# First batch's loads issued up front, transposes in three PSUM banks, a new split of the attention sums, and one held gate tile in an attention + gated-FFN kernel

## The chip, the cores and the metric

The kernel runs on one core of one Trainium2 chip. The metric is device time in microseconds (us), the median of several executions. Where a time within the kernel is given (such as "at 60.86 us"), it is read from one profiled execution and counts from the start of its span. The profiled span is about 1.7 us shorter than the device time.

## The reference, cut to what matters

```python
B, H, S, Nb, D = 8, 8, 576, 16, 64            # inputs float32
k_all = concatenate([beacon_k, k]); v_all = concatenate([beacon_v, v])      # 592 keys per head
scores = q @ k_all.T / sqrt(D)                # causal mask on the 576, never on the beacons
attn = softmax(scores) @ v_all                # per batch and head
x = attn.transpose(0, 2, 1, 3).reshape(B * S, H * D)                        # 4608 tokens x 512
out = (gelu(x @ w_gate) * (x @ w_val)) @ w_out                              # d_ff = 1536
```

## The kernel before

It works batch by batch: attention of batch b (four head pairs), then one 512-token chunk of gate and value work (12 tiles of 8 matmuls). The out-projection of the previous chunk (48 matmuls, "units", `o(n)`) is strewn through the attention, as filler while ScalarE computes the exps. Meanwhile GpSimd issues the casting loads of q, k and v for batch b+1, and SyncE issues ten DMA transposes that turn q and k into `qkT`, the operand of the scores.

The kernel's PSUM tiles take eight banks: `s` twice two banks (scores, gate/value tiles), `z` two banks, `x` one, `o` one.

```python
def attend(b, m, acc, c0, sums, q0, q1, start=True):       # columns q0..q1 of a pair's queries
    ...                                                    # per key tile and head one matmul:
    mm(acc[...], ones if sums else v_sb, expT, ...)

def sums(b, m):                                            # softmax sums, and the last 64 queries' values
    z_ps = psum_x.tile([P, 1024], FP32, tag="z")
    attend(b, m, z_ps, Z0 + Z_SPLIT, True, Z_SPLIT, S)     # 10 matmuls
    attend(b, m, z_ps, 0, False, X_SPLIT, S)               # 10 matmuls of 64 columns (X_SPLIT = 512)
    attend(b, m, z_ps, Z0, True, 0, Z_SPLIT, start=False)  # 2
def values(b, m):
    x_ps = psum_x.tile([P, X_SPLIT], FP32, tag="x")
    attend(b, m, x_ps, 0, False, 0, X_SPLIT)               # 10

def gate_val_first(ci, n=0):
    for fi in range(2):                                    # two tiles: both "s" buffers held
        gate_val_mms(ci, fi, range(K_CHUNKS - 1))
    o(n)                                                   # filler until the last pair is scaled
    for fi in range(2):
        gate_val_mms(ci, fi, [K_CHUNKS - 1])
        gate_val_end(ci, fi)                               # gelu on ScalarE, product on VectorE

# ... start: values first, then q/k runs
load_v_fp32(0)                                             # SyncE queue, fp32, cast later
heat(10)
load_runs(0, 2); load_beacon(dma, bk0, beacon_k[0]); ...; load_runs(2, 4)   # GpSimd queue
attention(0, "S0 r2 S1 k1 S2 q1 S3 r3 w0",                 # k, q: TensorE transposes through bank o
    "c024 S0 c13 S1 Z k2 I S2 V q2 w1 M S3", "S0 S1 Z k3 I w2 S2 V q3 M S3 w3",
    "S01 Z S2 V S3", "Z V", ...)                           # S scores, Z sums, I invert, V values, M scale
load_qk(1); load_v(1)                                      # r load q/k runs, w weights, c cast values
gate_val_first(0); xbar_transpose(1); gate_val(0, 2, F_TILES)
for b in range(1, B):
    if b == 1:   attention(b, "S0 L S1 S23", ..., "S0 S1 Z S2 V S3 O12", "Z V")  # L: w_out, O: units
    elif b == 2: attention(b, "S01 O12 S23 O12", "S01 Z V O12 S23 O12", ..., "Z V")   # 84 units
    else:        attention(b, "O4 S01 O8 S23 O2", "S01 Z V S23 O10", "S01 Z V S23 O12", "S01 Z V S23 O8", "Z V")
    load_qk(b + 1); load_v(b + 1)                          # (if b + 1 < B)
    gate_val_first(b, 4 if b > 2 else 0)
    xbar_transpose(b + 1)                                  # ten DMA transposes on SyncE
    gate_val(b, 2, F_TILES)
for fi in range(F_TILES): gate_val(8, fi, fi + 1); o(4)    # last chunk
o(OUT_UNITS)
```

The softmax here doesn't subtract the row's maximum and nothing guards it: scores larger than these inputs give would overflow.

Of the kernel before, what the change touches and what calls it, by code (L numbers as in the profile page):

```python
# [43 lines left out]
X_SPLIT = 512  # L44
Z0, Z_SPLIT = 448, 64
# [12 lines left out]
def kernel(  # L58
# [85 lines left out]
    def load_qk(b):  # L144

        qt, kt = q_ring[b % 2], k_ring[b % 2]
        load_beacon(dma, kt[0:NB, 0, :], beacon_k[b])

        def rows(dst, src):
            dma(dst.rearrange("p (h d) -> p h d", d=D), src.rearrange("h p d -> p h d"))  # L150

        for j in range(5):
            r0, n = (NB, 112) if j == 0 else (0, KROWS[j])
            rows(kt[r0 : r0 + n, j, :], k[b, :, S_LO[j] : S_LO[j] + n, :])
            n = min(P, S - j * P)
            rows(qt[0:n, j, :], q[b, :, j * P : j * P + n, :])
# [18 lines left out]
    def load_v_fp32(b):  # L175
        def start(o, i):
            keep(nc.sync.dma_start(out=o, in_=i))

        load_beacon(start, flat(v32)[0:NB, 0, :], beacon_v[b])
        for t in AV_ORDER:  # L180
            r0, n = (NB, 112) if t == 0 else (0, KROWS[t])
            start(v32[r0 : r0 + n, t, :, :], v[b, :, S_LO[t] : S_LO[t] + n, :].rearrange("h p d -> p h d"))

# [21 lines left out]
    def heat(n):  # L205
        t = psum_o.tile([P, CH], FP32, name="heat", tag="o")
        for _ in range(n):
            mm(t, warm[:, 0:P], warm, True, True)
# [31 lines left out]
    def trans_o(m, w, copy=None):  # L240
        t_ps = psum_o.tile([P, 1024], BF16, name="t_ps", tag="o")
        trans(m, w, t_ps, [(S, copy or dve_copy)])
# [56 lines left out]
    def sums(b, m):  # L299
        z_ps = z_of[b * NPAIR + m] = psum_x.tile([P, 1024], FP32, name="z_ps", tag="z")  # L300
        attend(b, m, z_ps, Z0 + Z_SPLIT, True, Z_SPLIT, S)
        attend(b, m, z_ps, 0, False, X_SPLIT, S)
        attend(b, m, z_ps, Z0, True, 0, Z_SPLIT, start=False)

    def values(b, m):
        x_ps = x_of[b * NPAIR + m] = psum_x.tile([P, X_SPLIT], FP32, name="x_ps", tag="x")
        attend(b, m, x_ps, 0, False, 0, X_SPLIT)

# [17 lines left out]
    def scale(b, m):  # L326
        i = b * NPAIR + m
        rec = rec_of.pop(i)
        del exp_of[i]
        for acc, q0, q1 in ((z_of.pop(i), X_SPLIT, S), (x_of.pop(i), 0, X_SPLIT)):  # L330
            keep(
                nc.vector.tensor_tensor(  # L332
                    out=xT_sb[:, m, b * S + q0 : b * S + q1],
                    in0=acc[:, 0 : q1 - q0],
                    in1=rec[:, q0:q1],
                    op=ALU.mult,
                )
            )
# [35 lines left out]
    def gate_val_first(ci, n=0):  # L374

        for fi in range(2):
            gate_val_mms(ci, fi, range(K_CHUNKS - 1))
        o(n)
        for fi in range(2):
            gate_val_mms(ci, fi, [K_CHUNKS - 1])  # L380
            gate_val_end(ci, fi)
# [31 lines left out]
    def attention(b, *slots, extra=None):  # L413


        for m, slot in enumerate(slots):
            for step in slot.split():
# [3 lines left out]
                elif kind == "Z":  # L421
                    sums(b, m - 1)
                    if "I" not in slot:
                        invert(b, m - 1)
                elif kind == "I":
                    invert(b, m - 1)
                elif kind == "V":
                    values(b, m - 1)
                    if "M" not in slot:
                        scale(b, m - 1)  # L430
                elif kind == "M":
                    scale(b, m - 1)
                elif kind == "O":
                    o(int(n))
                else:
                    extra[kind](*n)
# [4 lines left out]
    load_v_fp32(0)  # L441
# [15 lines left out]
    for w, copies in ((0, [(S, dve_copy)]), (1, [(114, act_copy), (S, act_copy)])):  # L457
        t0 = psum_s.tile([P, 2048], BF16, name="t0_ps", tag="s")
        trans(0, w, t0, copies)

    W_CUT = ((0, 256), (256, 512), (512, 1024), (1024, 1536))
    extra = {
        "k": lambda m: trans_o(int(m), 1),
        "q": lambda m: trans_o(int(m), 0),
        "c": lambda *tt: cast_v(0, *(int(t) for t in tt)),
        "r": lambda m: load_runs(2 * int(m), 2 * int(m) + 2),
        "w": lambda i: load_gate_val(*W_CUT[int(i)]),
# [3 lines left out]
        "S0 r2 S1 k1 S2 q1 S3 r3 w0", "c024 S0 c13 S1 Z k2 I S2 V q2 w1 M S3", "S0 S1 Z k3 I w2 S2 V q3 M S3 w3", "S01 Z S2 V S3", "Z V",  # L471
        extra=extra,
    )
    load_qk(1)
    load_v(1)
    gelu_table()
    gate_val_first(0)
# [3 lines left out]
    extra["L"] = load_out_w  # L481
    for b in range(1, B):
        exp_table()
        if b == 1:
            attention(b, "S0 L S1 S23", "S0 S1 Z S2 V S3", "S0 S1 Z S2 V S3", "S0 S1 Z S2 V S3 O12", "Z V", extra=extra)
        elif b == 2:
            attention(b, "S01 O12 S23 O12", "S01 Z V O12 S23 O12", "S01 Z V O12 S23 O12", "S01 Z V S23 O12", "Z V")
        else:
            attention(b, "O4 S01 O8 S23 O2", "S01 Z V S23 O10", "S01 Z V S23 O12", "S01 Z V S23 O8", "Z V")
# [4 lines left out]
        gate_val_first(b, 0 if b == 1 else 4 if b>2 else 0)  # L494
        if b + 1 < B:
            xbar_transpose(b + 1)
        gate_val(b, 2, F_TILES)
# [34 lines left out]
```

## Time and profile before

| | before |
|---|---|
| median time (three runs) | 426.18 us (426.07 to 426.87) |
| TensorE busy (profile, part 1) | 387.8 of 425.5 us, 91% |
| first scores / first gate matmul of batch 0 | 10.98 / 34.31 us |
| first scores of batch 1 | 59.36 us |
| first gate matmul of batches 1, 2, 3, 7 | 78.96, 132.56, 176.13, 353.30 us |
| batches 3 to 7, mean period | 44.3 us |

The occupancy rows of the profile (40 slices of 10.6 us, busy tenths; PEclk is the granted TensorE clock in tenths) show where TensorE has room: only at the front.

```profile
PE   5778958898999999999999999999999999999985
PEclk9589988999999999999999999999999999999999
```

The digits 5, 7, 7, 8 stand for batch 0, the 5 in the sixth slice is the wait before batch 1, and the PEclk digits 5 and 8 beside them say that the clock was also lowered there.

The waits view gives, for each pair of waiter and releaser, the total us, the count and the longest.

```profile
PE gv_ps L200 <- DVE hT_sb L364: 7.8, 8, 1.0
PE s_ps L200 <- DMA qkT<-q_sb: 3.5, 2, 3.0
```

The first line is a stall of 0.98 us in each of the eight batches: the third gate tile finds both PSUM buffers held. The second is small: transposed q is awaited for 3.0 us before batch 1 and 0.5 us once more.

The chain of work that ended last (start, us, what) names what set the pace at the front.

```profile
2.77 6.93 DMA bk<-in_beacon_k_dram
...
33.36 6.75 DMA k_sb<-in_k_dram
...
54.55 4.83 DMA qkT<-q_sb
59.38 0.39 PE s_ps L200 x2
```

Batch 1's chain is a load of k issued at 33.36 us (landing behind the weights at 40.1), ten transposes on SyncE, the last of which lands 4.8 us after its issue, and then the scores.

### The profile page before, as it was taken

To read this page: it belongs to the slowest core of one execution; us is meant where nothing else is said; L and a number is where in the kernel's file an instruction comes from. 1 tells how busy PE (TensorE), PEld (TensorE's weight loads), DVE (VectorE), ACT (ScalarE), POOL (GpSimd) and SP (SyncE) were. 2 spreads that over 40 slices of the span, in tenths; PEclk is the share of its full clock that TensorE was granted. 3 is DMA by queue.
4 is the path that set the end of the run, shared out by engine and by line. 5 is a ranking of instruction groups with operands and counts; after the bars stand their busy time and mean duration, and the time that the engine had idled before them with its cause. 6 is when DMAs were issued, how large, how long until landed. Compare 5 with 4: busy or idle time off the path is not lost.

```text
span 425.5 us, 7034 instructions
## 1 busy us (share of the span) xinstructions
PE 387.8 (91%) x2814; PEld 180.0 (42%) x2814; DVE 190.8 (45%) x324; ACT 188.6 (44%) x255; POOL 169.4 (40%) x302
## 2 busy tenths in 40 slices
PE   5778958898999999999999999999999999999985
PEld 2444424443444434444444444444544444444432
DVE  1565316533346335643564436444654365433321
ACT  1653368235343356435743476237723762322200
POOL 3868424930229504760468035813491230000000
PEclk9589988999999999999999999999999999999999
DMA  9599999995219991799149901991199310000111
GB/s 159 80 169 183 138 85 147 113 139 56 75 62 98 145 79 51 71 161 103 50 48 150 138 30 51 143 157 29 51 129 141 65 52 27 0 2 25 49 51 74
DMA packets 153041, 38.02 MB, mean 89 GB/s; under 512 B 141232, under 2 KB 148400, under 8 KB 153008
## 3 DMA queue, kind: packets, MB, share of 16 engines
q0 software_dynamic: 108048, 18.54, 64.7%
q1 hardware_dynamic: 44960, 19.03, 24.1%
q8 instruction: 22, 0.36, 0.4%
q14 instruction: 11, 0.09, 0.1%
HBM read 38.27 MB, written 9.44 MB: 112 GB/s over the span
## 4 chain that ended last, share of the span: by engine, by line
PE 71%; DMA 11%; SPq 7%; DVE 6%; ACT 3%; issue 2%; POOL 1%; DVEq 0%; ACTq 0%; POOLq 0%
PE gv_ps L200 33%; PE o_ps L200 22%; PE z_ps L200 7%; PE s_ps L200 6%; SPq L162 4%; PE x_ps L200 4%; DMA wo_sb<-in_moe_w_out_dram 3%; SPq L165 3%; DMA qkT<-q_sb 3%; DVE o_sb L402 2%; DVE hT_sb L364 2%; ACT ge_sb L203 2%; DMA bk<-in_beacon_k_dram 2%; DMA k_sb<-in_k_dram 2%; DMA qkT<-k_sb 1%
## 5 line engine op out<-in xcount | busy, mean ns | idle before, releaser
L203 ACT ACTIVATE ge_sb<-gv_ps 128x512 bf16<-128x512 f32 x108 | 63.6, 597 | 162.1 <-PE gv_ps L200 162.1
L271 POOL TENSOR_SCALAR_AFFINE_SELECT expT<-expT 128x256 bf16<-128x256 bf16 (+2 forms) x160 | 60.1, 387 | 168.5 <-ACT expT L203 168.2
L364 DVE TENSOR_TENSOR hT_sb<-gv_ps,ge_sb 128x512 bf16<-128x512 f32 x108 | 74.0, 691 | 117.4 <-ACT ge_sb L203 117.4
L203 ACT ACTIVATE expT<-s_ps 128x1024 bf16<-128x1024 f32 (+3 forms) x128 | 103.7, 862 | 46.8 <-PE s_ps L200 45.5
L200 PE MATMUL gv_ps<-xT_sb,wg_sb 128*128 128x512 bf16 x432 | 113.5, 379 | 7.8 <-DVE hT_sb L364 7.8
L200 PE MATMUL gv_ps<-xT_sb,wv_sb 128*128 128x512 bf16 x432 | 113.5, 379 | 0.0
L200 PE MATMUL o_ps<-wo_sb,hT_sb 128*128 128x512 bf16 x432 | 103.1, 379 | 7.0 <-DVE o_sb L402 6.2
L200 PEld LDWEIGHTS <-wg_sb 128*128 128x128 bf16 x432 | 41.6, 98 | 60.0 <-issue 11.8
L200 PEld LDWEIGHTS <-hT_sb 128*128 128x128 bf16 x432 | 40.2, 98 | 55.8 <-issue 11.6
L200 PEld LDWEIGHTS <-wv_sb 128*128 128x128 bf16 x432 | 42.3, 98 | 51.0
L200 PE MATMUL s_ps<-qkT 64*128 64x80 bf16 (+5 forms) x384 | 41.3, 296 | 12.6 <-DMA qkT<-q_sb 3.5
L402 DVE COPY o_sb<-o_ps 128x512 f32<-128x512 f32 x36 | 24.9, 691 | 53.9 <-PE o_ps L200 53.9
L315 DVE STREAM_TRANSPOSE zt<-z_ps 128x576 f32<-128x576 f32 x32 | 25.0, 782 | 40.6 <-PE z_ps L200 40.6
L200 PE MATMUL z_ps<-expT,ones 128*64 128x464 bf16 (+5 forms) x384 | 36.2, 300 | 1.1 <-DVE xT_sb L332 1.1
L112 POOL DMA_DIRECT2D v_sb<-in_v_dram x35 | 29.7, 869 | 10.9 <-DMA k_sb<-in_k_dram 5.7
L200 PEld LDWEIGHTS <-qkT 64*128 64x128 bf16 x384 | 14.7, 95 | 42.9 <-issue 28.9
L112 POOL DMA_DIRECT2D k_sb<-in_k_dram x35 | 30.2, 864 | 1.0 <-DMA wv_sb<-in_moe_w_val_dram 1.0
L112 POOL DMA_DIRECT2D q_sb<-in_q_dram x35 | 30.6, 874 | 0.0
L200 PEld LDWEIGHTS <-v_sb 128*64 128x64 bf16 (+1 forms) x640 | 22.0, 114 | 8.4 <-issue 2.6
L320 DVE STREAM_TRANSPOSE rec<-rz 128x576 f32<-128x576 f32 x32 | 24.9, 778 | 1.1
L200 PE MATMUL x_ps<-expT,v_sb 128*64 128x512 bf16 (+4 forms) x320 | 25.4, 285 | 0.0
L200 PEld LDWEIGHTS <-ones 128*64 128x64 bf16 (+1 forms) x384 | 17.6, 114 | 13.6 <-issue 9.0
(34 smaller groups left out, 115.4 us busy)
## 6 DMA issues: line engine op xcount, KB each, us to landing
out_dram<-o_sb SPq DMA_DIRECT2D x36, 256.0 KB, 2.0
q_sb<-in_q_dram POOLq DMA_DIRECT2D x28, 128.0 KB, 6.0
k_sb<-in_k_dram POOLq DMA_DIRECT2D x21, 128.0 KB, 6.1
v_sb<-in_v_dram POOLq DMA_DIRECT2D x21, 128.0 KB, 10.4
wo_sb<-in_moe_w_out_dram POOLq DMA_DIRECT2D x1, 1536.0 KB, 13.4
wg_sb<-in_moe_w_gate_dram POOLq DMA_DIRECT2D x2, 512.0 KB, 7.0
wv_sb<-in_moe_w_val_dram POOLq DMA_DIRECT2D x2, 512.0 KB, 8.9
k_sb<-in_k_dram POOLq DMA_DIRECT2D x7, 112.0 KB, 3.4
```

The source lines that it names most:

```text
L112: keep(nc.gpsimd.dma_start(out=out_ap, in_=in_ap))
L162: keep(nc.sync.dma_start_transpose(out=qkT[:, 1, :, j * P : j * P + n], in_=kt[0:n, j, :]))
L165: keep(nc.sync.dma_start_transpose(out=qkT[:, 0, :, c : c + n], in_=qt[0:n, j, :]))
L200: keep(nc.tensor.matmul(out_ap, lhsT, rhs, start=start, stop=stop, **kw))
L203: keep(nc.scalar.activation(out_ap, in_ap, func, **kw))
L271: nc.gpsimd.affine_select(out=d, in_=d, pattern=[[0, 2], [1, DIAG[t]]], compare_op=ALU.is_ge, fill=0.0, base=NB if t == 0 else 0, channel_ ...
L315: keep(nc.vector.transpose(zt, z_of[i][:, Z0 : Z0 + S]))
L320: nc.vector.transpose(rec.rearrange("p (n j) -> p n j", j=32), rz.unsqueeze(2).to_broadcast([P, NBLK, 32]))
L364: nc.vector.tensor_tensor(out=h_of[ci][:, fi, :], in0=gv_ps[:, 1, :], in1=ge_sb, op=ALU.mult)
L402: keep(nc.vector.tensor_copy(o_sb, o_ps))
```

## The change: its intent, and the diff

1. **First batch.** All q and k runs are loaded first; the fp32 values follow behind (a one-element GpSimd write to their tile holds SyncE back), and two of the five value tiles come by GpSimd's casting queue. TensorE's transposes rotate through banks o, x and z, one pair ahead. The weights come in three slices instead of four. A few warm-up matmuls keep the clock up.
2. **Output weights** (`L`) are loaded before batch 1's first scores instead of after them.
3. **Out-projections** move: batch 1 takes 24 units instead of 12, batch 2 60 instead of 84, the tail 12 more; batches 3 to 7 keep 48.
4. **One gate tile held** in batches 1 to 7 instead of two, with up to 7 units as filler.
5. **New split.** The first 64 queries, not the last 64, sit beside the sums. Only one key tile reaches them, so ten small matmuls become two.

In the schedule strings of the changed kernel, a digit after Z, I, V or M names the pair, `o` or `x` after k1, q1 and so on the PSUM bank, `y3` loads value tile 3 by GpSimd, and `N1` issues the next waiting load of batch 1.

```diff
-X_SPLIT = 512
-Z0, Z_SPLIT = 448, 64
+SPLIT = 64
+Z0 = 448
 ...
     def sums(b, m):
-        attend(b, m, z_ps, Z0 + Z_SPLIT, True, Z_SPLIT, S)
-        attend(b, m, z_ps, 0, False, X_SPLIT, S)
-        attend(b, m, z_ps, Z0, True, 0, Z_SPLIT, start=False)
+        attend(b, m, z_ps, Z0, True, 0, SPLIT)
+        attend(b, m, z_ps, Z0 + SPLIT, True, SPLIT, S)
+        attend(b, m, z_ps, 0, False, 0, SPLIT, start=False)
     def values(b, m):
-        attend(b, m, x_ps, 0, False, 0, X_SPLIT)
+        attend(b, m, x_ps, 0, False, SPLIT, S)
 ...
-    def gate_val_first(ci, n=0):
-        for fi in range(2):
+    def gate_val_first(ci, fill, n, tiles=1):
+        for fi in range(tiles):
             gate_val_mms(ci, fi, range(K_CHUNKS - 1))
-        o(n)
-        for fi in range(2):
+        fill(n)
+        for fi in range(tiles):
 ...
-    load_v_fp32(0)
     heat(10)
     load_runs(0, 2)
 ...
     load_runs(2, 4)
+    load_runs(4, 6)
+    load_runs(6, 8)
+    keep(nc.gpsimd.memset(v32[0:1, :, 0, 0:1], 0.0))
+    load_v_fp32(0)
 ...
-    W_CUT = ((0, 256), (256, 512), (512, 1024), (1024, 1536))
+    W_CUT = ((0, 512), (512, 1024), (1024, 1536))
     attention(0,
-        "S0 r2 S1 k1 S2 q1 S3 r3 w0", "c024 S0 c13 S1 Z k2 I S2 V q2 w1 M S3", "S0 S1 Z k3 I w2 S2 V q3 M S3 w3", "S01 Z S2 V S3", "Z V",
+        "S0 k1o q1x S1 S2 q2o S3 k2x y3 y4", "w0 N1 S0 c0 Z0 S1 S2 S3", "w1 I0 k3x c2 S0 c1 S1 q3o V0 M0 Z1 S2 V1 S3", "I1 S0 M1 S1 Z2 S2 S3 I2 V2 M2", "Z3 I3 V3 w2 M3",
 ...
-    gate_val_first(0)
+    gate_val_first(0, heat, 2, 2)
 ...
-            attention(b, "S0 L S1 S23", "S0 S1 Z S2 V S3", "S0 S1 Z S2 V S3", "S0 S1 Z S2 V S3 O12", "Z V", extra=extra)
+            attention(b, "L S0 S1 S2 S3", "S0 S1 Z0 S2 I0 S3 V0", "M0 Z1 S0 S1 O7 S2 V1 I1 S3 M1", "S0 Z2 S1 I2 V2 S2 S3 M2 O5", "Z3 I3 V3 M3 O12", extra=extra)
 ...                                    # batch 2 likewise, 84 units -> 60
-            attention(b, "O4 S01 O8 S23 O2", "S01 Z V S23 O10", "S01 Z V S23 O12", "S01 Z V S23 O8", "Z V")
+            attention(b, "O5 S0 S1 O7 S2 S3 O2", "S0 S1 Z0 I0 V0 S2 M0 S3 O10", "S0 S1 Z1 V1 I1 S2 S3 M1 O12", "S0 S1 Z2 V2 I2 M2 S2 S3 O5", "Z3 I3 V3 M3")
 ...
-        gate_val_first(b, 0 if b == 1 else 4 if b>2 else 0)
+        gate_val_first(b, o, 0 if b == 1 else 0 if b == 2 else 7)
 ...
-        gate_val(b, 2, F_TILES)
+        gate_val(b, 1, F_TILES)
+    o((N_CHUNKS - 2) * OUT_UNITS - out_done[0])
```

More of the change, by code (lines that the diff above doesn't have):

```diff
@@ L142, in load_beacon, with qk_loads, load_qk @@
         start(dst.rearrange("p (h d) -> p h d", d=D), src.rearrange("h p d -> p h d"))
-    def load_qk(b):
+    def qk_loads(b):
         qt, kt = q_ring[b % 2], k_ring[b % 2]
-        load_beacon(dma, kt[0:NB, 0, :], beacon_k[b])
         def rows(dst, src):
-            dma(dst.rearrange("p (h d) -> p h d", d=D), src.rearrange("h p d -> p h d"))
+            return dst.rearrange("p (h d) -> p h d", d=D), src.rearrange("h p d -> p h d")
+        loads = [rows(kt[0:NB, 0, :], beacon_k[b])]
         for j in range(5):
             r0, n = (NB, 112) if j == 0 else (0, KROWS[j])
-            rows(kt[r0 : r0 + n, j, :], k[b, :, S_LO[j] : S_LO[j] + n, :])
+            loads.append(rows(kt[r0 : r0 + n, j, :], k[b, :, S_LO[j] : S_LO[j] + n, :]))
             n = min(P, S - j * P)
-            rows(qt[0:n, j, :], q[b, :, j * P : j * P + n, :])
+            loads.append(rows(qt[0:n, j, :], q[b, :, j * P : j * P + n, :]))
+        return loads
+    def load_qk(b):
+        for out_ap, in_ap in qk_loads(b):
+            dma(out_ap, in_ap)
     def xbar_transpose(b):
@@ L179, in load_v_fp32, with load_v_tile @@
         load_beacon(start, flat(v32)[0:NB, 0, :], beacon_v[b])
-        for t in AV_ORDER:
+        for t in (0, 2, 1):
             r0, n = (NB, 112) if t == 0 else (0, KROWS[t])
             start(v32[r0 : r0 + n, t, :, :], v[b, :, S_LO[t] : S_LO[t] + n, :].rearrange("h p d -> p h d"))
+    def load_v_tile(b, t):
+        dma(v_ring[b % 2][0 : KROWS[t], t, :, :], v[b, :, S_LO[t] : S_LO[t] + KROWS[t], :].rearrange("h p d -> p h d"))
     def cast_v(b, *tiles):
@@ L203, in act, with bank, heat @@
         keep(nc.scalar.activation(out_ap, in_ap, func, **kw))
-    def heat(n):
-        t = psum_o.tile([P, CH], FP32, name="heat", tag="o")
+    def bank(tag, dtype, n, name):
+        pool = psum_o if tag == "o" else psum_x
+        if tag == "z":
+            n *= 2
+        return pool.tile([P, n], dtype, name=name, tag=tag)
+    def heat(n, tag="o"):
+        if n == 0:
+            return
+        t = bank(tag, FP32, CH, "heat")
         for _ in range(n):
-            mm(t, warm[:, 0:P], warm, True, True)
+            mm(t[:, 0:CH], warm[:, 0:P], warm, True, True)
     def tr(out_ap, in_ap):
@@ L238, in act_copy, with trans_in @@
         keep(nc.scalar.copy(o, i))
-    def trans_o(m, w, copy=None):
-        t_ps = psum_o.tile([P, 1024], BF16, name="t_ps", tag="o")
+    def trans_in(tag, m, w, copy=None):
+        t_ps = bank(tag, BF16, 1024, "t_ps")
         trans(m, w, t_ps, [(S, copy or dve_copy)])
@@ L300, in sums @@
         z_ps = z_of[b * NPAIR + m] = psum_x.tile([P, 1024], FP32, name="z_ps", tag="z")
-        attend(b, m, z_ps, Z0 + Z_SPLIT, True, Z_SPLIT, S)
-        attend(b, m, z_ps, 0, False, X_SPLIT, S)
-        attend(b, m, z_ps, Z0, True, 0, Z_SPLIT, start=False)
+        attend(b, m, z_ps, Z0, True, 0, SPLIT)
+        attend(b, m, z_ps, Z0 + SPLIT, True, SPLIT, S)
+        attend(b, m, z_ps, 0, False, 0, SPLIT, start=False)
     def values(b, m):
-        x_ps = x_of[b * NPAIR + m] = psum_x.tile([P, X_SPLIT], FP32, name="x_ps", tag="x")
-        attend(b, m, x_ps, 0, False, 0, X_SPLIT)
+        x_ps = x_of[b * NPAIR + m] = psum_x.tile([P, S - SPLIT], FP32, name="x_ps", tag="x")
+        attend(b, m, x_ps, 0, False, SPLIT, S)
     rec_of = {}
@@ L329, in scale @@
         del exp_of[i]
-        for acc, q0, q1 in ((z_of.pop(i), X_SPLIT, S), (x_of.pop(i), 0, X_SPLIT)):
+        for acc, q0, q1 in ((z_of.pop(i), 0, SPLIT), (x_of.pop(i), SPLIT, S)):
             keep(
@@ L421, in attention @@
                 elif kind == "Z":
-                    sums(b, m - 1)
-                    if "I" not in slot:
+                    sums(b, int(n or m - 1))
+                    if not n:
                         invert(b, m - 1)
                 elif kind == "I":
-                    invert(b, m - 1)
+                    invert(b, int(n))
                 elif kind == "V":
-                    values(b, m - 1)
-                    if "M" not in slot:
+                    values(b, int(n or m - 1))
+                    if not n:
                         scale(b, m - 1)
                 elif kind == "M":
-                    scale(b, m - 1)
+                    scale(b, int(n))
                 elif kind == "O":
@@ L435, in attention @@
                 else:
-                    extra[kind](*n)
+                    extra[kind](*n) if kind in "kqcrwLhy" else extra[kind](n)
     exp_table()
-    load_v_fp32(0)
     heat(10)
@@ L456, with load_next @@
     load_runs(2, 4)
-    for w, copies in ((0, [(S, dve_copy)]), (1, [(114, act_copy), (S, act_copy)])):
+    load_runs(4, 6)
+    load_runs(6, 8)
+    keep(nc.gpsimd.memset(v32[0:1, :, 0, 0:1], 0.0))
+    load_v_fp32(0)
+    for w, copies, n in ((0, [(S, dve_copy)], 0), (1, [(114, act_copy), (S, act_copy)], 3)):
         t0 = psum_s.tile([P, 2048], BF16, name="t0_ps", tag="s")
         trans(0, w, t0, copies)
-    W_CUT = ((0, 256), (256, 512), (512, 1024), (1024, 1536))
+        heat(n)
+    queue = qk_loads(1)
+    def load_next(n):
+        for _ in range(min(n, len(queue))):
+            dma(*queue.pop(0))
+    W_CUT = ((0, 512), (512, 1024), (1024, 1536))
     extra = {
-        "k": lambda m: trans_o(int(m), 1),
-        "q": lambda m: trans_o(int(m), 0),
+        "k": lambda m, tag: trans_in(tag, int(m), 1),
+        "q": lambda m, tag: trans_in(tag, int(m), 0),
         "c": lambda *tt: cast_v(0, *(int(t) for t in tt)),
         "r": lambda m: load_runs(2 * int(m), 2 * int(m) + 2),
+        "h": lambda n, tag: heat(int(n), tag),
+        "L": lambda: load_out_w(),
+        "y": lambda t: load_v_tile(0, int(t)),
+        "X": lambda n: load_v(1),
+        "N": lambda n: load_next(int(n)),
         "w": lambda i: load_gate_val(*W_CUT[int(i)]),
@@ L470 @@
         0,
-        "S0 r2 S1 k1 S2 q1 S3 r3 w0", "c024 S0 c13 S1 Z k2 I S2 V q2 w1 M S3", "S0 S1 Z k3 I w2 S2 V q3 M S3 w3", "S01 Z S2 V S3", "Z V",
+        "S0 k1o q1x S1 S2 q2o S3 k2x y3 y4", "w0 N1 S0 c0 Z0 S1 S2 S3", "w1 I0 k3x c2 S0 c1 S1 q3o V0 M0 Z1 S2 V1 S3", "I1 S0 M1 S1 Z2 S2 S3 I2 V2 M2", "Z3 I3 V3 w2 M3",
         extra=extra,
     )
-    load_qk(1)
+    load_next(99)
     load_v(1)
     gelu_table()
-    gate_val_first(0)
+    gate_val_first(0, heat, 2, 2)
     xbar_transpose(1)
     gate_val(0, 2, F_TILES)
-    extra["L"] = load_out_w
     for b in range(1, B):
@@ L484 @@
         if b == 1:
-            attention(b, "S0 L S1 S23", "S0 S1 Z S2 V S3", "S0 S1 Z S2 V S3", "S0 S1 Z S2 V S3 O12", "Z V", extra=extra)
+            attention(b, "L S0 S1 S2 S3", "S0 S1 Z0 S2 I0 S3 V0", "M0 Z1 S0 S1 O7 S2 V1 I1 S3 M1", "S0 Z2 S1 I2 V2 S2 S3 M2 O5", "Z3 I3 V3 M3 O12", extra=extra)
         elif b == 2:
-            attention(b, "S01 O12 S23 O12", "S01 Z V O12 S23 O12", "S01 Z V O12 S23 O12", "S01 Z V S23 O12", "Z V")
+            attention(b, "S0 O12 S1 S2 O12 S3", "S0 Z0 I0 S1 S2 O12 S3 V0 M0", "S0 S1 Z1 I1 V1 S2 S3 O6", "S0 S1 M1 Z2 V2 S2 S3 O4 I2 M2", "O2 Z3 V3 I3 M3 O12", extra=extra)
         else:
-            attention(b, "O4 S01 O8 S23 O2", "S01 Z V S23 O10", "S01 Z V S23 O12", "S01 Z V S23 O8", "Z V")
+            attention(b, "O5 S0 S1 O7 S2 S3 O2", "S0 S1 Z0 I0 V0 S2 M0 S3 O10", "S0 S1 Z1 V1 I1 S2 S3 M1 O12", "S0 S1 Z2 V2 I2 M2 S2 S3 O5", "Z3 I3 V3 M3")
         gelu_table()
```

## The prediction

> **What bounds the kernel now.** TensorE. By the profile's first part it is busy 387.8 of 425.5 us; from batch 3 on, batches repeat every 44.2 us with it nearly full. The losses:
> - Start (timeline): the first scores run at 10.98 us, because the beacon keys issued at 2.77 us land 6.93 us later, among the fp32 value loads. The exps of batch 0 go from 11.63 to 32.40 us, 20.8 us for about 14 us of work (862 ns x 16): they wait for transposes that pass one by one through one PSUM bank. Gate work starts at 34.31.
> - Batch 1 starts at 59.36 us after 3.0 us of waiting for transposed q, whose chain begins with loads landing behind the weights (40.14 us). The clock is at half for 9.0-19.3, 22.7-26.1 and 60.2-67.0 us.
> - Each batch: 0.98 us where the third gate tile waits for a PSUM buffer, since two are held open (waits: 8 times, 7.8 us).
> - Batch 2: 84 out-projection units, with stalls (1.09 + 3 x 0.39 us).
>
> **What the change is worth.**
> 1. q/k runs first, values behind them. A q or k load alone landed in 3.1 us (6-7 under the value loads); my estimate for the first scores is 7.3 us, 3.5 earlier. Transposes in three banks, one pair ahead, let ScalarE run nearly without gaps (perhaps 5 more): last exp near 24, gate work near 25.5. The warm-up matmuls should avoid the half-clock stretch from 9 us. The Trainium skill, "TensorE: Matmul & The Clock Gate", Part 1, says that the clock drops after an idle window of about 3.4 us; the clock records agree (stretches of 3.4, 6.8, 10.2 us).
> 2. But batch 1 is tied to DMA: 3.1 MB of weights at the 205 GB/s seen, 11 loads, ten DMA transposes (19.2 us from first issue to last landing). The weights start some 4 us earlier. The output weights now load beside the transposes; the Trainium skill, "DMA: Bandwidth & Descriptors", "Issuing engines are not separate DMA queues", says that these share the 16 engines, so I charge 1-2 us. Batch 1 starts at about 53.5: **-5.9**. TensorE still waits there some 5 us; the clock still drops.
> 3. Out-projections: batch 1 takes 24 units instead of 12 in the same time (filling waits), batch 2 60 instead of 84 (-5.2, and -1.8 of stalls), the tail 12 more (+2.6).
> 4. One held gate tile in batches 1-7: 7 x 0.98 = **-6.9**.
> 5. The split saves 8 matmuls per pair: ten 64-column ones (0.15 us together, timeline) become two; the large group keeps about 0.7 us. -0.12 x 24 pairs where TensorE is the limit = **-2.9**.
> 6. Score waits at batch starts: -1.0. New waits (scores for exps, transposed keys; slack there is about 1 us): +1.2.
>
> Sum -19.9: 426.2 becomes **407 us**, with 400 to 414 holding it 8 times in 10. Faster by over 2%: 0.95; within 2%: 0.045; slower: 0.005.
>
> **What would show it.** First scores near 7 us; last exp of batch 0 near 24; batch 1's first scores at 52-55 after a DMA wait; period near 42.4 us; the 0.98 us gate stalls gone but for batch 0's; z and x groups 0.12 us shorter per pair.
>
> **What would make it wrong.** Output weights delaying the transposes so that batch 1 starts near 59 as before (+5); later batches limited by the DMA chain, the stalls reappearing as waits for transposed keys.

## The result, and the profile after

The changed kernel takes 419.54 us (median of 4, 419.40 to 420.15) against 426.36 us for the kernel before in the same rounds. The ratio is 0.9842, with a 95% interval of 0.9824 to 0.9859. Ratios here and below are the mean time of one kernel's fast runs over that of the other's of the same rounds, so they are not quite the ratio of the quoted medians. The change is a gain of 1.6%; 407 us, or 4.5%, had been predicted.

Marks read from the timelines (first gate matmul of a batch, and the scores that open batch 1) divide the difference:

| stretch | before | after | difference | predicted |
|---|---|---|---|---|
| start to gate of batch 0 | 34.31 | 28.21 | -6.1 | -8.8 |
| start to the scores of batch 1 with all data | 59.36 | 60.86 | +1.5 | -5.9 |
| from there to gate of batch 1 | 19.6 | 20.1 | +0.5 | 0 |
| gate of batch 1 to gate of batch 2 | 53.6 | 45.4 | -8.2 | about -8.5 |
| gate of batch 2 to gate of batch 7 | 220.7 | 217.0 | -3.8 | about -7 |
| gate of batch 7 to the end | 72.2 | 74.4 | +2.2 | about +1.6 |

The first row is part of the second; rows two to six sum to -7.8 us, against the -19.9 of the prediction. (The last column sorts the terms of its sum by row. The fifth is five stalls, 4.9, and 20 pairs of the split, 2.4, less 0.2 for waits; the period of 42.4 us that the prediction also names would make it -9.) Most of the miss of 12 us is in two rows, 7.4 us before batch 1 and about 3 us in batches 2 to 6; the other three are off by 0.3 to 0.6 us each. Batch 0 did get 6.1 us faster, and all of it is lost again before batch 1.

The occupancy rows of the changed kernel:

```profile
PE   7789819999999989998999999989999999999975
PEclk9899967999999999999999999999999999999999
```

The third and fourth digit rose to 8 and 9, but the sixth, before batch 1, fell from 5 to 1, and PEclk stands at 6 and 7 there.

The waits view:

```profile
PE s_ps L209 <- DMA qkT<-q_sb: 7.4, 5, 3.3
PE s_ps L209 <- issue: 6.2, 1, 6.2
PE gv_ps L209 <- DVE hT_sb L382: 1.0, 1, 1.0
```

The gate stall went from 7.8 us in 8 to 1.0 in 1, just as intended. What grew is the wait for transposed q, from 3.5 us in 2 to 7.4 in 5, and one of 6.2 us which the view cannot attribute ("issue"). The stretch itself shows what that one is (timeline of TensorE and SyncE, 50 to 62 us; lines between left out):

```profile
49.65 1.03 PE L209 MATMUL gv_ps<-xT_sb,wv_sb 128*128 128x512 bf16 x4
...
51.05 1.20 SPq L171 DMA_TRANSPOSE qkT<-q_sb  x1
...
56.91 0.61 PE L209 MATMUL s_ps<-qkT 64*128 64x512 bf16 x2 [6.23 <-issue]
...
60.86 0.97 PE L209 MATMUL s_ps<-qkT 64*128 64x64 bf16 x8 [3.35 <-DMA qkT<-q_sb]
```

Gate work of batch 0 ends at 50.7 us, and TensorE then waits 6.23 and 3.35 us. The chain of the changed kernel for this stretch:

```profile
28.00 8.81 DMA k_sb<-in_k_dram
36.83 1.30 SPq L168
...
51.05 9.77 DMA qkT<-q_sb
```

The load of k was issued 5.4 us earlier than before but landed only 3.3 us earlier, at 36.8. The last transpose took 9.77 us to land where it had taken 4.83. The clock was lowered for longer, too: half speed from 54.5 to 68.1 us, 13.7 us, against 6.8 us before (60.2 to 67.0).

In batches 3 to 7 the removed stalls came back as waits of another name. TensorE's waits at the head of batches 3, 4, 6 and 7 (start of the matmul, us, and in brackets the idle time before it):

```profile
149.58 0.38 PE L209 MATMUL s_ps<-qkT 64*128 64x64 bf16 x6 [0.94 <-DMA qkT<-q_sb]
192.79 0.60 PE L209 MATMUL s_ps<-qkT 64*128 64x512 bf16 x8 [0.78 <-DMA qkT<-q_sb]
280.06 0.38 PE L209 MATMUL s_ps<-qkT 64*128 64x64 bf16 x6 [0.81 <-DMA qkT<-q_sb]
324.35 0.38 PE L209 MATMUL s_ps<-qkT 64*128 64x64 bf16 x6 [1.52 <-DMA qkT<-q_sb]
```

So the working theories were: **A**, the output weights, now moved beside the transposes, delay batch 1; **F**, batch 1 is tied to the queue of loads, so that a faster batch 0 is worth little; **C**, in batches 3 to 7 the chain of loads and transposes stood at its limit already, so that stalls taken from TensorE turn into waits for it. The rivals are given with each run.

### The profile page after: what moved, and what is told of

Read it like the earlier page. It is cut to its first block, busy times and chain, and to the rows that moved or that the text cites. A ratio compares the mean times of both kernels' runs of the same rounds, so it can differ in the third digit from the quotient of the medians.

```text
span 417.7 us, 6524 instructions
## 1 busy us (share of the span) xinstructions
PE 385.3 (92%) x2563; PEld 175.8 (42%) x2563; DVE 191.5 (46%) x322; ACT 189.8 (45%) x255; POOL 168.4 (40%) x303
## 4 chain that ended last, share of the span: by engine, by line
PE 69%; DMA 13%; SPq 9%; DVE 2%; POOL 2%; ACT 2%; issue 1%; DVEq 0%; POOLq 0%
PE gv_ps L209 29%; PE o_ps L209 22%; DMA qkT<-q_sb 10%; PE s_ps L209 7%; PE z_ps L209 6%; SPq L168 5%; PE x_ps L209 5%; SPq L171 4%; DMA k_sb<-in_k_dram 2%; DVE o_sb L420 2%; ACT expT L212 2%; DMA v<-in_v_dram 1%; POOL q L113 1%; POOL k L113 0%; POOL expT L289 0%
## 5 line engine op out<-in xcount | busy, mean ns | idle before, releaser
L209 PE MATMUL gv_ps<-xT_sb,wv_sb 128*128 128x512 bf16 x432 | 112.3, 379 | 0.0
L113 POOL DMA_DIRECT2D v_sb<-in_v_dram x37 | 31.5, 869 | 16.2 <-DMA q_sb<-in_q_dram 15.4
L209 PEld LDWEIGHTS <-qkT 64*128 64x128 bf16 x384 | 14.7, 95 | 49.2 <-issue 35.1
L209 PE MATMUL z_ps<-expT,ones 80*64 80x80 bf16 (+5 forms) x384 | 30.2, 292 | 1.0 <-POOL expT L289 0.7
L209 PE MATMUL x_ps<-expT,v_sb 128*64 128x512 bf16 (+4 forms) x320 | 28.8, 311 | 0.0
L350 DVE TENSOR_TENSOR xT_sb<-x_ps,rec 128x512 bf16<-128x512 f32 x32 | 21.8, 682 | 1.5 <-PE x_ps L209 1.5
L209 PEld LDWEIGHTS <-ones 128*64 128x64 bf16 (+1 forms) x384 | 15.5, 112 | 14.3 <-issue 8.0
## 6 DMA issues: line engine op xcount, KB each, us to landing
wo_sb<-in_moe_w_out_dram POOLq DMA_DIRECT2D x1, 1536.0 KB, 19.2
```

Source lines behind the costliest of these rows:

```text
L113: keep(nc.gpsimd.dma_start(out=out_ap, in_=in_ap))
L209: keep(nc.tensor.matmul(out_ap, lhsT, rhs, start=start, stop=stop, **kw))
L350: nc.vector.tensor_tensor(out=xT_sb[:, m, b * S + q0 : b * S + q1], in0=acc[:, 0 : q1 - q0], in1=rec[:, q0:q1], op=ALU.mult,)
```

## The experiments

The kernel before ran beside every group; its medians there were 425.94 to 426.65 us. For batches 3 to 7 a measure without the start is the time from the gate of batch 3 to that of batch 7, four batches, in one profile. Before: 177.17 us; after: 174.78. It repeats within 1.5 us: the four other kernels below that leave this stretch as the change made it (output weights late, values first, sums later, q and k first) took 175.97 to 176.27. The marks at the front repeat less well. In the changed kernel and the four below that leave its front alone (transposes ahead, loads during the attention, two tiles held, the control of the last group), the transposes of batch 1 began between 35.4 and 36.8 us, and the scores of batch 1 with all data ran between 58.4 and 62.5.

### Output weights late again (after, one letter moved)

```diff
-attention(b, "L S0 S1 S2 S3", ...)
+attention(b, "S0 L S1 S2 S3", ...)
```

> The changed kernel, but the output weights are loaded after the first scores of batch 1, as in the kernel before. Theory A (the output weights share the DMA engines with the transposes of batch 1 and delay them): the last transposed q tile, issued at 51.05 us and landing 9.8 us later, now lands within about 5 us; the scores that need it run at 54 to 56 us instead of 60.86. The first out-projections then wait several us for the output weights, so the total gains only 0 to 5 us. Rival B (the transposes are late for their own reasons: serial issue, loads behind the weights): those scores still run at 59 to 61 us.

Measured: 422.94 us, ratio 0.9919. That is 3.3 us worse than the changed kernel, outside what I expected for the total. For the mechanism the expectation held: all scores of batch 1 could run at 56.03 us, without a second wait.

```profile
56.03 1.07 PE L209 MATMUL s_ps<-qkT 64*128 64x512 bf16 x8 [5.94 <-issue]
...
71.32 3.15 PE L209 MATMUL o_ps<-wo_sb,hT_sb 128*128 128x512 bf16 x7 [5.41 <-DMA wo_sb<-in_moe_w_out_dram]
```

The output weights beside the transposes cost 4.8 us (60.86 against 56.03), so theory A is right as far as it goes. A single mark could be chance, but the stretch from the first transpose of batch 1 to its scores with all data separates the kernels: 18.2 to 19.4 us in the five that load the output weights after the first scores (the kernel before and its two variants, this run, and one run of the last group), 22.5 to 25.9 us in the eight that load them beside the transposes with the other weights ahead. But the units that the change put into batch 1 need these weights, and here they wait 5.41 us for them. The early load is therefore a trade that this schedule needs. And 56.03 is still 2.5 us later than the 53.5 predicted: A is not the whole cause.

### Transposes ahead of the first gate tile (after, two statements swapped)

```diff
-        gate_val_first(b, o, 0 if b == 1 else 0 if b == 2 else 7)
-        if b + 1 < B:
-            xbar_transpose(b + 1)
+        if b + 1 < B:
+            xbar_transpose(b + 1)
+        gate_val_first(b, o, 0 if b == 1 else 0 if b == 2 else 7)
```

> The changed kernel, but in each batch the transposing DMAs stand ahead of the first gate tile in program order instead of behind it, so that SyncE does not hold them behind the store of the output tile that the fill of that gate tile finishes. Theory C (in batches 3 to 7 the chain of loads and transposes is now the limit; the removed PSUM stalls came back as waits for transposed q and k, 4 us in all in batches 3 to 7): the first transposes of a batch are issued 2 to 4 us earlier, most of these waits go, total 2 to 4 us shorter than the changed kernel. Rival D (the chain is limited by the loads, issued by GpSimd and moved at 150 GB/s, not by when the transposes may begin): waits stay at 3 to 4 us, total within 1 us.

Measured: 414.05 us, ratio 0.9717, 5.3 us better than the changed kernel. Four batches take 171.10 us, 3.7 to 5.2 less than in the kernels that keep the change's stretch. After the head of batch 3 (0.90 us) no wait for `qkT` is left. In the changed kernel, SyncE first takes the store of the output tile that the filler finishes (batch 3, SyncE's timeline):

```profile
172.27 0.33 SPq L422 DMA_DIRECT2D out_dram<-o_sb  x1
172.78 1.32 SPq L168 DMA_TRANSPOSE qkT<-k_sb  x1
174.19 1.73 SPq L171 DMA_TRANSPOSE qkT<-q_sb  x1
176.01 2.98 SPq L168 DMA_TRANSPOSE qkT<-k_sb  x1
...
187.63 1.20 SPq L171 DMA_TRANSPOSE qkT<-q_sb  x1
```

and with the two swapped:

```profile
171.09 1.20 SPq L168 DMA_TRANSPOSE qkT<-k_sb  x1
...
184.25 1.20 SPq L171 DMA_TRANSPOSE qkT<-q_sb  x1
185.54 0.53 SPq L422 DMA_DIRECT2D out_dram<-o_sb  x1
```

The gate of this batch began at 168.53 and 167.94 us, so relative to it the first transpose is issued 1.1 us earlier (3.15 instead of 4.25) and the last one 2.8 us earlier (16.3 instead of 19.1). The transposes take as long as before to land (median 7.1 to 7.2 us, against 7.7); only their issue moved. Theory C holds. The gain was more than the 2 to 4 us that I had written down.

### Loads during the attention (after)

```diff
+        if b > 1 and b + 1 < B:
+            queue.extend(qk_loads(b + 1))
 ...
-            attention(b, "O5 S0 S1 O7 S2 S3 O2", "S0 S1 Z0 I0 V0 S2 M0 S3 O10", "S0 S1 Z1 V1 I1 S2 S3 M1 O12", ...)
+            attention(b, "O5 S0 S1 O7 S2 S3 N3 O2", "S0 S1 Z0 I0 V0 S2 M0 S3 N3 O10", "S0 S1 Z1 V1 I1 S2 S3 N3 M1 O12", ...)
 ...                                    # N3: issue three loads; batch 2 likewise
-            load_qk(b + 1)
+            load_qk(b + 1) if b == 1 else load_next(99)
```

> The changed kernel, but from batch 2 on nine of the eleven q and k loads of the next batch are issued during the attention, three per pair, instead of after it; the transposes stay where they are. Theory C with the loads as its limit (rival D above): the transposes find their data, each is issued 1.3 us after the other without the 2 to 3 us pauses, waits for transposed q and k in batches 4 to 7 vanish, total 3 to 4 us shorter than the changed kernel. If the transposes' own start and pace are the limit: waits stay, total within 1 us. If GpSimd becomes late with the masks of the exps: z groups wait for it and the total grows.

Measured: 414.61 us, ratio 0.9718; four batches in 171.08 us. The same limit was reached by the other end of the chain: the transposes start where they did, but with the loads out of their way they land in a third of the time. The DMA view (us to landing, median) for batch 3, first the changed kernel, then this one:

```profile
qkT<-k_sb SPq DMA_TRANSPOSE x5, 7.7
qkT<-q_sb SPq DMA_TRANSPOSE x5, 7.7
```

```profile
qkT<-k_sb SPq DMA_TRANSPOSE x5, 3.1
qkT<-q_sb SPq DMA_TRANSPOSE x5, 2.4
```

So neither "they start too late" nor "the loads are slow" is the one true limit. It is one chain of loads and transposes that share the DMA engines, and slack given to it at either end removes the wait.

### Two tiles held again (after)

```diff
-        gate_val_first(b, o, 0 if b == 1 else 0 if b == 2 else 7)
+        gate_val_first(b, o, 0 if b == 1 else 0 if b == 2 else 7, 2)
 ...
-        gate_val(b, 1, F_TILES)
+        gate_val(b, 2, F_TILES)
```

> The changed kernel, but in batches 1 to 7 two gate tiles are held open again, with the same out-projection units as fill. The PSUM stall of 0.98 us comes back 7 times. Theory C (in batches 3 to 7 the removed stall only became a wait for the transposes): the total grows by only 2 to 4 us over the changed kernel, as the waits for transposed q and k shrink. Rival (the stalls are worth their full length): it grows by 6 to 7 us.

Measured: 423.78 us, ratio 0.9921, 3.4 us more than the changed kernel. The stall is back (7.8 us in 8), the waits for `qkT` after batch 1 shrink to 0.22 and 0.48 us, and four batches take 176.32 us: +1.5 for 3.9 us of stall. The account closes: 3.92 us of stall came, 2.41 us of waits went (3.11 to 0.70). Against the four other kernels with this stretch as changed (175.97 to 176.27) the stall even cost next to nothing. This is theory C from the other side; the rival's 6 to 7 us are refuted.

### One tile held, alone, in the kernel before

```diff
-    def gate_val_first(ci, n=0):
-        for fi in range(2):
+    def gate_val_first(ci, n=0, tiles=2):
+        for fi in range(tiles):
 ...
-            attention(b, "O4 S01 O8 S23 O2", "S01 Z V S23 O10", "S01 Z V S23 O12", "S01 Z V S23 O8", "Z V")
+            attention(b, "O5 S01 O7 S23 O2", "S01 Z V S23 O10", "S01 Z V S23 O12", "S01 Z V S23 O5", "Z V")
 ...
-        gate_val_first(b, 0 if b == 1 else 4 if b>2 else 0)
+        gate_val_first(b, 7 if b > 2 else 0, 1 if b > 2 else 2)
 ...
-        gate_val(b, 2, F_TILES)
+        gate_val(b, 1 if b > 2 else 2, F_TILES)
```

> The kernel before with one part of the change alone: in batches 3 to 7 one gate tile is held open instead of two, with the change's placing of the out-projections (5, 7, 2, 10, 12, 5 and 7 as fill). Five PSUM stalls of 0.98 us go. Theory C (already before the change the chain of loads and transposes stood within about half a microsecond of the limit): waits for transposed q and k grow in batches 4 to 7, the total falls by 1 to 3 us. Rival (TensorE's own work is the limit): the total falls by 5 us or more.

Measured: 423.71 us, ratio 0.9951 (0.9924 to 0.9978), 2.1 us of the 4.9 that five stalls make up. Four batches: 175.48 us, -1.7 for 3.9 us of stall. Waits for `qkT` of 0.89, 0.72 and 1.46 us appear in batches 5, 6 and 7. In the four batches these waits grew from 0.66 to 3.07 us while 3.92 us of stall went: the kernel before already stood at the limit of the chain, with about 0.4 us of slack per batch.

### The split, alone, in the kernel before

The edit is the hunk for `sums` and `values` shown in the diff, with the two ranges in `scale` swapped to match.

> The kernel before with the new split alone (the first 64 queries beside the sums instead of the last 64; eight matmuls fewer per pair). TensorE saves 0.12 us per pair, 2.9 us over batches 2 to 7, if it is the limit. Theory C: part of it comes back as waits for transposed q and k, the total falls by 0.5 to 2 us. Rival: it falls by 3 us or more.

Measured: 423.73 us, ratio 0.9949 (0.9926 to 0.9973), 2.2 us less. But the split hardly made it: four batches take 176.76 us, only 0.4 less, and the waits for `qkT` did not grow. Half of the profiled run's lead of 3.2 us was already there at the gate of batch 0 (32.67 us against 34.31), three quarters at the scores of batch 1 (56.97 against 59.36), and its first scores, which come before any use of the split, ran 1.0 us earlier. Whether that lead is chance of the DMA landings stays open. What the split is worth is read from TensorE's timeline of one pair in a full stretch, first before, then after:

```profile
218.74 0.88 PE L200 MATMUL z_ps<-expT,ones 128*64 128x512 bf16 x10
219.45 0.32 PE L200 MATMUL z_ps<-expT,v_sb 128*64 128x64 bf16 x10
219.60 0.20 PE L200 MATMUL z_ps<-expT,ones 128*64 128x64 bf16 x2
219.63 0.77 PE L200 MATMUL x_ps<-expT,v_sb 128*64 128x512 bf16 x10
220.33 0.82 PE L200 MATMUL gv_ps<-xT_sb,wg_sb 128*128 128x512 bf16 x3
```

```profile
210.41 0.91 PE L209 MATMUL z_ps<-expT,ones 128*64 128x64 bf16 x12
211.15 0.20 PE L209 MATMUL z_ps<-expT,v_sb 128*64 128x64 bf16 x2
211.18 0.85 PE L209 MATMUL x_ps<-expT,v_sb 128*64 128x512 bf16 x10
211.97 0.82 PE L209 MATMUL gv_ps<-xT_sb,wg_sb 128*128 128x512 bf16 x3
```

From start to start, the ten small matmuls (0.15 us) become two (0.03), but the large group grows from 0.70 to 0.79 us, because its ten matmuls now carry the columns that moved. One pair goes from 1.59 to 1.56 us: 0.03 saved, not the 0.12 predicted.

### Values first again (after)

```diff
     exp_table()
+    load_v_fp32(0)
     heat(10)
 ...
-    keep(nc.gpsimd.memset(v32[0:1, :, 0, 0:1], 0.0))
-    load_v_fp32(0)
```

> The changed kernel, but the fp32 values of batch 0 are loaded at the very start again, beside q and k, instead of behind them. If ordering is what brings the first scores forward: they run at 9.5 to 11 us instead of 7.71, and the wait of the sums group for the cast values (1.5 us at 14.69) goes. Since batch 1 starts only when DMA delivers, I expect the gate work of batch 0 within 2 us of 28.2 and the total within 2 us of the changed kernel, on the slower side.

Measured: 423.42 us, ratio 0.9931 with a wide interval (0.9869 to 0.9992; its runs spread from 420.1 to 425.4). First scores at 10.97 us, as expected; gate at 30.61, 2.4 us later than in the changed kernel; the scores of batch 1 with all data at 64.49, 3.6 us later. The total grew by about 4 us, not by under 2. The scores of batch 1 lie 2 us beyond the latest of the five kernels with the change's front (62.45), so the order of the loads is a part of the change's gain, though how large is uncertain: one of the four runs, 420.1 us, was as fast as the changed kernel. Delaying the front does delay batch 1: GpSimd, which issues the weights, first waits for exps to mask (first mask at 12.72 us instead of 9.24), issues the first weights at 17.61 us instead of 14.36, and the transposes begin at 38.62 instead of 36.83.

### Sums later (after)

```diff
-        "w0 N1 S0 c0 Z0 S1 S2 S3"
+        "w0 N1 S0 S1 S2 c0 Z0 S3"
```

> The changed kernel, but in batch 0 the first sums group with its cast of the first value tile stands behind two more score groups, so that TensorE does not wait for late values. The wait of 1.5 to 2.2 us for the cast values shrinks below 0.3 us, gate work of batch 0 starts 1 to 2 us earlier than 28.2. Theory F (batch 1 is tied to the queue of loads, above all to the weights, and not to the end of batch 0): batch 1's delayed scores move by less than 1 us and the total by less than 1 us. Rival (batch 1 follows batch 0): the total falls by 1 to 2 us.

Measured: 418.54 us, ratio 0.9839 (0.9796 to 0.9882), the same as the changed kernel. The run did not do what it was built for. The sums' wait for the cast values did go (0.6 us of it is left, at the values), but a gap of 3.46 us before an exp opened elsewhere, and the gate came 1.2 us later (29.44), not earlier. As a test of F it still says something: the gate came later, yet the transposes of batch 1 began at 36.74 us (36.83 in the changed kernel) and the scores with all data ran at 59.26, within the spread of this mark. Batch 1 does not follow the end of batch 0.

### q and k of batch 1 ahead of the last weights (after)

```diff
-        ..., "Z3 I3 V3 w2 M3",
+        ..., "Z3 I3 V3 M3",
 ...
     load_next(99)
+    load_gate_val(*W_CUT[2])
     load_v(1)
```

> The changed kernel, but the q and k loads of batch 1 are issued ahead of the last third of the gate and value weights (needed by gate tile 8, at about 42 us) instead of behind it. Theory F (the place of these loads in the queue, behind 3.1 MB of weights, sets when batch 1 can start: the transposes began at 36.6 to 36.8 us in three kernels whose gate work began at 27.6 to 29.4): the transposes begin at 30 to 32 us, the scores of batch 1 that need the last q tile run at 51 to 55 us instead of 60.86, TensorE's 9.6 us of waiting before them shrinks to under 4 us, total 5 to 9 us shorter than the changed kernel. Rival G (what delays them is the output weights alone): the transposes begin earlier, but the last one still lands at about 60 us, total within 2 us.

Measured: 417.53 us, ratio 0.9786, 2.4 us better than the changed kernel (one slow run of five, 423.45 us, is left out). The transposes now begin at 30.32 us, and no score of batch 1 waits for `qkT`. But the gate tiles wait for the weights that were put back:

```profile
44.91 1.04 PE L209 MATMUL gv_ps<-xT_sb,wg_sb 128*128 128x512 bf16 x4 [0.74 <-DMA wg_sb<-in_moe_w_gate_dram]
48.79 1.89 PE L209 MATMUL gv_ps<-xT_sb,wv_sb 128*128 128x512 bf16 x4 [2.84 <-DMA wv_sb<-in_moe_w_val_dram]
```

The scores that had been delayed run at 58.02 us, 2.8 earlier, not the 6 to 10 expected, and hardly earlier than in the control below (58.43). The order in the queue decides who waits, more than how long: gate work now ends at about 56.5 us instead of 50.7.

### All three remedies (after)

> The changed kernel with the three remedies together: q and k of batch 1 ahead of the last weights, transposes ahead of the first gate tile, and from batch 2 on nine of eleven q and k loads issued during the attention. If the two causes (the queue at batch 1, the chain of loads and transposes in batches 3 to 7) are separate, their gains add: 5 to 9 us and 5.3 us, total 405 to 410 us, with batches of 42.8 us and no wait for transposed q or k after batch 1.

The edit is the sum of the last one and of the two for batches 3 to 7. Measured: 413.83 us, ratio 0.9722 (0.9699 to 0.9745). The gains did not add: this is what either of the steady-state remedies gives alone. Batches take 42.77 us each, but gate tiles wait 4.1 us for weights (2.11 and 1.97). Against the control of the next group, which has both steady-state remedies and the change's order at the front (0.9686), this run is 1.5 us slower, with intervals that just overlap: beside the other two, q and k ahead of the weights brought no gain.

### Filling the queue earlier, and taking the output weights away

Three kernels, all with both steady-state remedies; the third is their control and has nothing else. The first issues the second and third weight slice one pair earlier each. The second does so too, and loads the output weights late, with the 12 units of batch 1's attention moved behind it.

```diff
-        "w0 N1 S0 c0 Z0 S1 S2 S3", "w1 I0 k3x ...", ..., "Z3 I3 V3 w2 M3",
+        "w0 w1 N1 S0 c0 Z0 S1 S2 S3", "w2 I0 k3x ...", ..., "Z3 I3 V3 M3",
 ...                                    # second kernel only:
-            attention(b, "L S0 S1 S2 S3", ..., "M0 Z1 S0 S1 O7 S2 V1 I1 S3 M1", "S0 Z2 S1 I2 V2 S2 S3 M2 O5", "Z3 I3 V3 M3 O12")
+            attention(b, "S0 S1 L S2 S3", ..., "M0 Z1 S0 S1 S2 V1 I1 S3 M1", "S0 Z2 S1 I2 V2 S2 S3 M2", "Z3 I3 V3 M3 O12 O12")
```

> The changed kernel with transposes ahead of the first gate tile and loads during the attention (the third kernel of this group), and besides the second and third parts of the gate and value weights issued one pair earlier each (at about 16 and 18 us instead of 18 and 26.5), so that the queue does not run dry at 16 to 18 and at 28 us. If the queue of loads sets batch 1's start: the transposes of batch 1 begin at 32 to 34 us instead of 36.7, the delayed scores of batch 1 run at 56 to 58 us instead of 60.3, no gate tile waits for weights, total 2 to 4 us below the third kernel. If not: no difference beyond 1 us.

> As the first kernel of this group, but the output weights are loaded after two score groups of batch 1, and the 12 out-projections inside its attention are moved to its end, so that nothing waits for these weights and nothing of them lies beside the transposes. If the output weights cost the transposes 4.5 us, as the run with late output weights showed: batch 1's delayed scores run at 51 to 53 us; the 12 out-projections at the end cost up to 2.6 us, so total 1 to 3 us below the first kernel of this group, 407 to 410 us. If something else holds the transposes: scores stay at 56 to 58 us and the total rises by 2 us.

> Control for the two kernels above: the changed kernel with both remedies of batches 3 to 7 (transposes ahead of the first gate tile, nine of eleven loads during the attention). Each alone brought the period to 42.77 us, where TensorE does not wait. If both removed the same wait, together they bring no more than one: within 1 us of either, about 414 us.

| | median us | ratio (95%) | transposes of batch 1 begin | scores of batch 1 with all data |
|---|---|---|---|---|
| control | 413.08 | 0.9686 (0.9653 to 0.9720) | 35.42 | 58.43 |
| weights early | 412.92 | 0.9687 (0.9645 to 0.9729) | 35.52 | 59.41 |
| weights early, output weights late | 412.53 | 0.9659 (0.9615 to 0.9703) | 35.19 | 54.30 |

The control did as expected: both remedies together are worth no more than one. Issuing weights earlier changed nothing (in the first kernel the third slice was issued at 19.3 us instead of 26.3, and the transposes began no sooner). In the control the queue did run low: 98 GB/s from 26 to 30 us, where the first kernel moved 204. But the first kernel moved less at the start (134 GB/s up to 18 us, the control 186), and the last weights landed at about 34.7 us in both. So filling the gap in the queue gained nothing here; whether the slower start comes from the earlier issue was not tested. Taking the output weights out of the way brings the scores to 54.30 us, 5.1 earlier than in the first kernel, which differs in nothing else at the front, and 4.1 earlier than in the control. This confirms A a second time, though 51 to 53 us had been expected for this run, and 407 to 410 for its total, which it missed:

```profile
54.30 1.01 PE L209 MATMUL s_ps<-qkT 64*128 64x512 bf16 x8 [4.04 <-DMA qkT<-k_sb]
```

In the total, though, it is worth 0.5 us of medians (the intervals overlap): the 12 units that no longer fill the attention of batch 1 stand behind it, and the gate of batch 1 begins at 78.51 us against 78.54 in the control. These three kernels beat both the kernel before and the changed one, by about 13.5 and 7 us, and cannot be told apart in time.

## Why the prediction was right or wrong

- **One held gate tile** ("7 x 0.98 = -6.9"): the stalls vanished as said, and their size was right. That they would shorten the kernel by their length was wrong. In the stretch of four batches, putting the stall in or out moved the time by at most 1.7 us for 3.9 us of stall (two tiles held again; one held in the kernel before). The failed step is that the prediction let TensorE alone set the period. With the DMA chain relieved, a batch takes 42.77 us, near the 42.4 predicted, which fits a stall worth its length once nothing else binds; two held tiles with the chain relieved were not run.
- **New waits** ("slack there is about 1 us ... +1.2"): this is the first failed step, the other side of the same error. The kernel before had about 0.4 us of slack per batch, and waits of 0.45 and 0.66 us in batches 3 and 5 said so. The waits for `qkT` at the heads of batches 3 to 7 sum to 4.05 us in the changed kernel and to 4.4 to 5.2 in the four others that keep its stretch; both ways of relieving the chain brought 5.3 us.
- **Batch 1's start** ("-5.9"): the second failed step, 7.4 us off. It has two parts. The output weights were charged "1-2 us" and cost 4.8 (and 4.1 to 5.1 in the last group); here the mechanism was right and the term too small. The other part is the passage of the weights, taken "at the 205 GB/s seen", which is 15 us for 3.1 MB. The 53.5 us, less the 19.2 of the transposes and the 1 to 2 charged, need transposes that begin near 33 us; they began at 36.83, and between 35.2 and 36.8 in the other kernels that load the values last and the weights before q and k. The 3.1 MB took 21.7 us from the first issue at 14.4 to the last landing at 36.1 us, 145 GB/s on average. The kernel before could have told: there it was 21.3 us, from 17.98 to 39.3. Its first and last weight issue (GpSimd's timeline, lines between left out; the last landed 10.4 us after its issue), then those of the changed kernel (the last landed after 8.8 us):

```profile
17.98 0.78 POOL L112 DMA_DIRECT2D wg_sb<-in_moe_w_gate_dram  x1
...
28.91 0.75 POOL L112 DMA_DIRECT2D wv_sb<-in_moe_w_val_dram  x1
```

```profile
14.36 0.77 POOL L113 DMA_DIRECT2D wg_sb<-in_moe_w_gate_dram  x1
...
27.27 0.76 POOL L113 DMA_DIRECT2D wv_sb<-in_moe_w_val_dram  x1
```

  So the transposes began earlier only by about what the weights were issued earlier (3.4 and 3.6 us). 205 GB/s is a rate of single stretches and of all traffic together: in the changed kernel it is 118 GB/s from 14 to 18 us and 166 to 202 after, q and k of batch 1 and the values included. Why so little moves in those first 4 us, with the engines busy and the fp32 values among the traffic, was not tested.
- **Batch 0** ("gate work near 25.5"): 28.21. First scores at 7.71 were as predicted (7.3), and the clock was at half for 3.4 us (17.1 to 20.5) instead of 13.7. TensorE waited 1.5 us for the values, which landed 6.1 us after their issue at 7.96 us. Moving that wait away (sums later) opened another gap. In any case the run with sums later shows that the end of batch 0 does not set the start of batch 1.
- **The split** ("-0.12 x 24 pairs = -2.9"): mis-sized, 0.03 us per pair, 0.7 us in all. The step that failed is "the large group keeps about 0.7 us": it grew to 0.79.
- **Out-projections** ("-5.2, and -1.8 of stalls", "+2.6"): right. The stretch of batch 2 shrank by 8.2 us.
- **The clock.** The Trainium skill, "TensorE: Matmul & The Clock Gate", Part 1, gives an idle window of about 3.4 us after which the clock is halved. The changed kernel agrees: TensorE fell idle at about 50.7 us, the clock at 54.5. But shorter gaps were enough elsewhere. In the kernel before the clock fell at 60.2 us after a wait of 3.0 us, with TensorE busy for 0.60 of the last 3.4 us; in the run with all three remedies it fell at 49.2 us after waits of 2.1 and 2.0 us, with TensorE busy for 1.04 of the last 3.4. The window need not be wholly idle; how much work keeps the clock up was not tested. With the longer wait before batch 1 the stretch at half clock doubled, from 6.8 to 13.7 us; in the other runs too it is longest where the waits are (17.1 us after waits of 8.5 and 3.3). That the clock drops there was predicted, that it does so for longer was not.
- **Sharing of DMA engines.** The Trainium skill, "DMA: Bandwidth & Descriptors", "Issuing engines are not separate DMA queues", says that transfers interleave on the same 16 engines whoever issues them. The runs agree, with numbers: a transpose lands in 2.4 to 3.1 us when the loads are out of the way, in 7.7 beside them, and the last one of batch 1 in 9.8 beside the output weights. Knowing the rule did not help to size it; only the experiments did.

The prediction did name both failures ("output weights delaying the transposes", "the stalls reappearing as waits for transposed keys") but gave them too little weight.

## What to carry to other kernels

When one engine looks 91% busy, a second chain may stand right behind it: before counting a removed stall as gain, look in every period for how late the next stage's operand lands, and take small scattered waits (here 0.45 and 0.66 us) as a sign that there may be no slack. A load that is moved forward takes bandwidth from whatever was there; ask which transfer it now runs beside, and price it by that transfer's landing time under load, not alone. Price a long load by the time that its like took in the profile, first issue to last landing (here 21.3 us), not by the best rate in it (here it gave 15). Where a chain binds, its place in an in-order queue may be the cheapest remedy: swapping two statements brought 5.3 us, nearly as much as the whole change.

## What the Trainium skill lacked or had wrong

- "DMA: Bandwidth & Descriptors" ("Latency and other measured facts") gives a bandwidth for DMA transposes but no landing time beside other traffic: here 2.4 to 3.1 us with the loads issued earlier, 7.7 us beside loads, 9.8 us beside the output weights; nor, but for cycle counts of "previous generations" in its table on trn3 B0, the issuing engine's time: here at least 1.2 us of SyncE for each issue, and 13.1 us for ten that never had to wait (batch 3, loads during the attention).
- The same page ("Issuing engines are not separate DMA queues") says that starting DMAs from several engines at once only saves sequencer time, usually small beside the transfer. It has nothing on what the order within one engine's queue can cost: moving the transposes ahead of a store issued the last of them 2.8 us earlier and made the kernel 5.3 us faster.
- "TensorE: Matmul & The Clock Gate" ("Back-to-back issue gap") gives about 131 ns per matmul of 512 columns in a sustained stream of weight loads and matmuls. Here four such matmuls with 128x128 weights take 0.86 us from start to start (182.46 to 183.32 us in the kernel before), 215 ns each, which is that page's figure for the isolated gap. (On its idle window, see the clock above.)
